# Probabilities stationary and V moving in the PV product of a decode-attention kernel

## The chip, the core and the metric

The kernel runs on one core of one Trainium2 chip. The core has five engines with in-order instruction streams of their own: TensorE (PE in the profile, with its weight loads as PEld), VectorE (DVE), ScalarE (ACT), GpSimd (POOL) and SyncE (SP, which here only issues DMAs). The metric is the device time of one execution in microseconds (us); lower is better. Times of several runs of one kernel are given by their median.

## The reference

Two rounds of the same two layers, with the same weights and the same caches in both rounds, for 8 sequences of one new token each:

```python
x = x + A(layernorm(x))      # grouped-query attention over a cache, then wo
x = x + B(layernorm(x))      # silu MLP
x = x + A(layernorm(x))
x = x + B(layernorm(x))

def A(x):                    # B=8, D=512, Hq=32, Hkv=8 (REP = 4 query heads per kv head), Sk=8192, Dh=128
    q = (x @ wq) in heads
    scores = q . k_cache * Dh**-0.5
    p = softmax(scores, over Sk)
    return (p . v_cache in heads) @ wo
```

K and V hold 8 sequences x 8 kv heads x 8192 keys x 128 values each in bf16, 2 MiB per sequence and kv head in each of K and V. Both rounds read all of them.

## The kernel before

One *task* is one round (`layer` 0 or 1), one sequence b and one kv head g: 128 tasks in all. A task has four steps of 2048 keys, so there are 512 steps, counted by `c`. A step's K and V pieces are 512 KB each, and lie in slots of an on-chip store, `ARENA`, of 28 slots (`NSLOT`). A piece has 128 partitions x 2048 values: 16 chunks of 128 keys.

Of each sequence, the K pieces of the last five kv heads (20 slots, `KEEP`) stay in the store from round 0 to round 1. The order of the tasks (`make_tasks`) therefore goes per sequence: five tasks of round 0 whose K is kept, some tasks of other rounds and sequences that load everything while the kept K occupies 20 of the slots, then the five tasks of round 1 that use the kept K and load V alone. I call the steps of these last five tasks **kept steps** (40 tasks, 160 steps in all), and the others **streaming steps**.

SP issues the loads in the order of need. A load waits until the instruction that last read its slot has finished; how far SP goes at which step is set by `issue_until`.

In a streaming step the main loop (L873 to L913) emits, in this order:

- `emit_t` twice: TensorE transposes 8 chunks of K each time into one of three PSUM banks `TPp` (L474), and ScalarE (first half, L480) or VectorE (second half, L482) copies them back over the piece
- pieces of the softmax of earlier tasks: `softmax_exp` (VectorE L520, L522, then ScalarE L524 writes the probabilities `P`), `softmax_sum` (VectorE L530, GpSimd L532), `softmax_rcp` (VectorE L549)
- `emit_pv` of step c-6 (`LAG`): P times V for a task before
- at one step in four, where c leaves the remainder 1 on division by 4: `emit_norm` (VectorE L574) of the task whose last PV has just been emitted, and `emit_pt`, which transposes the next task's `P` on TensorE (L540) and copies it into `PT` on VectorE (L544)
- `emit_s`: the scores of step c (L500). Four matmuls with the query stationary, 32 columns each, and 512 keys moving, in four column tiles of TensorE (`tile_position=(0, t * QR)`)
- `softmax_max` after the last scores of a task (VectorE L511, L513, GpSimd L515)

In a kept step there are no transposes, and the scores are emitted ahead of the PV. After the last round-0 task of each sequence a *chain* of small steps (wo, layer norm, MLP, next queries) is threaded through the following steps.

The operations of each engine run in the order in which they are emitted. `op` gives an instruction the waits for what it reads and writes, by name (`reads`, `writes`); on VectorE also those on VectorE's own earlier results.

The PV product before: the V chunk (128 keys x 128 values) is the stationary operand, and the moving operand is the chunk's probabilities of four heads, each repeated 8 times (32 columns). A step has 16 weight loads and 16 matmuls; all 64 of a task add into one small area of the PSUM bank `OTp`, which then holds the output of four heads, values on partitions. `emit_norm` is one VectorE multiplication by 1 / sum. What ends the step before the first PV of the next task is therefore one small VectorE operation.

Of the kernel before, what the change touches and what calls it, by code (L numbers as in the profile page):

```python
# [7 lines left out]
DH = 128  # L8
# [5 lines left out]
GRP = 8  # L14
HALVES = 2
SPT = 4
# [15 lines left out]
INT32 = mybir.dt.int32  # L32
ACT = mybir.ActivationFunctionType
ALU = mybir.AluOpType
AX = mybir.AxisListType
# [202 lines left out]
def _build(ctx, nc, A_x, A_k_cache, A_v_cache, A_wq, A_wo, B_w1, B_w2, out):  # L238
    B, _sq, D = A_x.shape
# [14 lines left out]
    tasks = make_tasks(B, HKV, (len(order) - KEEP) // NGRAN)  # L254
# [5 lines left out]
    pe = nc.tensor  # L260
    dve = nc.vector
# [41 lines left out]
    assert KB == D  # L303
    P = sb([128, KB], BF16, "P")
    Xr = P
    PT = sb([128, CPB, NT, NGRAN * REP], BF16, "PT")
    small = sb([128, 4 * REP + 23 * NST + 5 * B + 2 * KT + FT], FP32, "small")
    taken = [0]

    def few(n):  # L310
        o = taken[0]
        taken[0] += n
        assert taken[0] <= small.shape[-1]
        return small[:, o:o + n]

    hm, hneg, hsc, nbr = [few(REP) for _ in range(4)]
    mxr, mxa, ssm, ssa, rcp = [[few(REP) for _ in range(NST)] for _ in range(5)]
    mxp, nb, rs = [[few(1) for _ in range(NST)] for _ in range(3)]
    vr, yr, tr, s1, s1a = [few(B) for _ in range(5)]
    last_use = [max(d.free for d in loads if d.slot <= s < d.slot + d.n) for s in range(NSLOT)]  # L320
    spare = last_use.index(min(last_use))

    def apart(space, shapes):
        o, got = 0, []
        for shape, dt in shapes:
            n = math.prod(shape) * (2 if dt == FP32 else 1)
            v = space[:, o:o + n]
            o += n
            v = v.bitcast(FP32) if dt == FP32 else v
            got.append(v.rearrange("p (k b) -> p k b", b=shape[1]) if len(shape) == 2 else v)  # L330
        assert o <= space.shape[-1]
        return got
# [1 line left out]
    one = (few(KT).unsqueeze(2), few(KT).unsqueeze(2), tiny[:, 0:KT].unsqueeze(2), "1")  # L334
    eh, hsT = few(FT), tiny[:, KT:KT + FT]
    rows8 = ((KT, B), FP32), ((KT, B), FP32), ((KT, B), BF16)
    opens = tuple(apart(PT[:, :, :, :].rearrange("p c t q -> p (c t q)"), rows8)) + (None,)
    *ends, ones, ehN, thN, hsN, XF, XO = apart(
        ARENA[:, spare * SLOT:(spare + 1) * SLOT],
        rows8 + (((128,), BF16), ((FT * B,), FP32), ((FT * B,), FP32), ((FT * B,), BF16), ((KT * B,), BF16), ((KT * B,), BF16)))  # L340
# [3 lines left out]
    OTp = ps_bank("OTp")  # L344
    UP = ps_bank("UP")
    TPp = [ps_bank("TPp", BF16) for _ in range(NTP)]
# [62 lines left out]
    with nc.Block() as block:  # L409

        @block.sync
        def _(sync_eng):
# [9 lines left out]
                reads=["ident"], writes=["ident"],  # L422
            )
            for n in range(NQB):
# [4 lines left out]
                    hm[:, :], ident[:, :].rearrange("p (t r k) -> p r t k", t=NT, k=NGRAN)[:, 0:REP], AX.XY, ALU.add),  # L429
                reads=["ident"], writes=["hm"],  # L430
            )
            op(dve, lambda: dve.tensor_scalar(hneg[:, :], hm[:, :], -1.0, MASKED, op0=ALU.add, op1=ALU.mult),
               reads=["hm"], writes=["hneg"])
            op(dve, lambda: dve.tensor_scalar(hsc[:, :], hm[:, :], -SM_SCALE, None, op0=ALU.mult),
# [100 lines left out]
            def emit_pt(ti):  # L535
                tb = evacs[0] % NTP
                evacs[0] += 1
                tpv = TPp[tb][:, 0:KB].rearrange("p (c q) -> p c q", q=128)
                steps = [
                    lambda c=c: pe.transpose(tpv[:, c, :], P[:, c * 128:(c + 1) * 128], ident[:, :])  # L540
                    for c in range(CPB)
                ]
                mm_group(steps, reads=["P", "ident"], writes=[f"TP{tb}"])
                op(dve, lambda: dve.tensor_copy(  # L544
                    PT[:, :, :, :], tpv.rearrange("p c (t q) -> p c t q", q=QR)[:, :, :, 0:NGRAN * REP]), reads=[f"TP{tb}"], writes=["PT"])

            def softmax_rcp(ti):
                st = ti % NST
# [2 lines left out]
            def emit_pv(c):  # L551
                ti = c // SPT
                _l, b, g, k = where(c)
                slot = v_slot[(b, g, k)]
                otp = OTp[:, 0:REP * PVN].rearrange("p (r n) -> p r n", n=PVN)
                steps = []
                for n in range(HALVES * GRP):
                    cc = k * HALVES * GRP + n
                    steps.append(
                        lambda n=n, cc=cc: pe.matmul(  # L560
                            otp, chunk(slot, n), PT[:, cc % CPB, (cc // CPB) % NT, cc // (CPB * NT)::NGRAN].unsqueeze(2).to_broadcast([128, REP, PVN]),
                            start=(cc == 0), stop=(cc == NCH - 1),
                        )
                    )
                mm_group(steps, reads=[r_half(slot, 0), r_half(slot, 1), "PT"], writes=["OT"])

            def emit_norm(ti):
                layer, b, g = tasks[ti]
                st = ti % NST
                if layer == 0:  # L570
                    dst, rd = at1[b % 3][:, g * REP:(g + 1) * REP], f"at1_{b % 3}"
                else:
                    dst, rd = QA[:, b, g * REP:(g + 1) * REP], f"QA{b}"
                op(dve, lambda: dve.tensor_tensor(dst, OTp[:, 0:REP * PVN:PVN], rcp[st][:, :], ALU.mult),  # L574
                   reads=["OT", f"rcp{st}"], writes=[rd])

            def ln_stages(xv, rx, n, bufs):
                xcv, sqv, xnv, tag = bufs
# [235 lines left out]
            def add_rest(b):  # L814
                while heads[b]:
                    add_heads(b)
# [35 lines left out]
            last0 = {b: max(task_at[(0, b, g)] for g in range(HKV)) for b in range(B)}  # L852
            first1 = {b: min(task_at[(1, b, g)] for g in range(HKV)) * SPT for b in range(B)}
            ntask = len(tasks)
            first = min(g for g, _k in kept)

            def step(kind):
                if chain and chain[0][0] == kind:
                    chain.pop(0)[1]()
                    return True  # L860
                return False

            def soft(c, f):
                if 0 <= c < NC and c % SPT == 0:
                    f(c // SPT)
# [7 lines left out]
            for c in range(NC + LAG):  # L873
                if c < NC:
                    layer, b, g, k = where(c)
                if c and c % SPT == 0 and c < NC:
                    assert layer == 0 or not chain or chain_b[0] != b
                    emit_q(c // SPT)
                ready = c < NC and (c < SPT or layer == 1 and (g, k) in kept)
                if ready:  # L880
                    scores(c)
                else:
                    emit_t(c, 0)
                    emit_t(c, 1)
                soft(c - SPT, softmax_exp)
                soft(c - SPT - 1, softmax_sum)
                soft(c - SPT - 2, softmax_rcp)
                step(MID)
                if 0 <= c - LAG:
                    emit_pv(c - LAG)  # L890
                    if (c - LAG) % SPT == SPT - 1:
                        emit_norm((c - LAG) // SPT)
                issue_until(2 * c)
                soft(c - SPT - 1, emit_pt)
                if turn[0] == B and not chain and heads[B]:
                    add_heads(B)
# [5 lines left out]
                if c >= LAG and (c - LAG) % SPT == SPT - 1:  # L902
                    tj = (c - LAG) // SPT
                    layer, b, g = tasks[tj]
                    if layer == 0:
                        heads[b].append(g)
                    elif b == B - 1:
                        heads[B].append(g)
                    if layer == 0 and tj == last0[b]:
                        assert not chain and turn[0] == b  # L910
                        chain.extend([(TILE, lambda b=b: add_rest(b))] + chain_of(b))
                        chain_b[0] = b
                        turn[0] = b + 1  # L913
            assert not queue and not chain

            rest = closing(B)
# [37 lines left out]
```

## Time and profile before

| what | value |
|---|---|
| runs | 1150.9, 1144.49, 1144.27 us; median 1144.49 us |
| the profiled execution | 1147.56 us; its span 1145.8 us |
| granted TensorE clock, mean | 0.929 |
| DMA traffic | 459.43 MB, mean 401 GB/s |
| PV matmuls L560 | 8192, 291.9 us busy |
| PV weight loads L560 | 8192, 250.6 us busy |
| score matmuls L500 | 2048, 220.7 us busy |
| K transposes L474 | 5632, 393.8 us busy |
| normalization L574 | 128, 20.1 us busy |

The span is the time from the first to the last instruction of the profiled execution. In a line of the timeline the first number is the start (us from the span's start), the second the duration in us; then engine, line, operation, what it writes and reads with shapes, the number of merged instructions, and in brackets the idle time of the engine before it with what ended it. In a line of a group, "busy" is total time and the number after it the mean duration in ns of one instruction.

### The profile page before, as it was taken

The numbers are of one execution on the slowest core, as the hardware profiler recorded it, in microseconds if no ns is written. First come the engines' busy times: TensorE is split into PE (matmuls) and PEld (weight loads), VectorE is DVE, ScalarE is ACT, GpSimd is POOL, SyncE is SP. The second block draws the span as 40 slices with busy tenths as digits, with TensorE's granted clock in tenths as the row PEclk, the third lists the DMA queues.
The fourth block names the chain that finished last, engine by engine and source line by source line (L and its number), as shares of the span: only waits on it lengthen the run. The fifth ranks groups of instructions, "written<-read, shape, count | busy, mean of one in ns | idle before, by whom it ended". The sixth has DMA issues, their size and how long they took to land.

```text
span 1145.8 us, 42536 instructions
## 1 busy us (share of the span) xinstructions
PE 926.5 (81%) x18616; PEld 697.2 (61%) x18616; DVE 536.3 (47%) x1702; ACT 471.5 (41%) x747; POOL 117.6 (10%) x300
## 2 busy tenths in 40 slices
PE   2868888888888887888788888888878888888886
PEld 2656665666566665766466655666566655666565
DVE  1334553445534553446434553446444553456433
ACT  1344441454335542554235542554245432554332
POOL 0000111001100011001100111001100011011110
PEclk9889997899879998999889997999889998999877
DMA  9999999999999999999999999999999999999994
GB/s 371 394 395 415 395 404 416 418 412 390 414 418 415 392 405 417 418 409 395 409 419 414 369 379 418 419 410 393 415 418 415 394 407 418 417 404 396 413 418 200
DMA packets 100334, 459.43 MB, mean 401 GB/s; under 512 B 10541, under 2 KB 16437, under 8 KB 73781
## 3 DMA queue, kind: packets, MB, share of 16 engines
q1 hardware_dynamic: 100132, 456.70, 99.2%
q8 instruction: 147, 2.41, 0.9%
q14 instruction: 39, 0.31, 0.1%
q10 hardware_dynamic: 16, 0.01, 0.0%
HBM read 456.66 MB, written 0.01 MB: 399 GB/s over the span
## 4 chain that ended last, share of the span: by engine, by line
DMA 66%; PE 21%; DVE 6%; SPq 3%; issue 2%; ACT 0%; POOL 0%; POOLq 0%; ACTq 0%; DVEq 0%
DMA arena<-in_A_v_cache_dram 53%; DMA arena<-in_A_k_cache_dram 11%; PE TPp L474 10%; DVE arena L482 5%; PE OTp L560 4%; PE SCp L500 4%; SPq L378 3%; DMA wo<-in_A_wo_dram 3%; PE MISC L678 2%; PE TPp L540 0%; DVE small L549 0%; DVE small L530 0%; PE MISC L650 0%; SPq L84 0%; DVE small L520 0%
## 5 line engine op out<-in xcount | busy, mean ns | idle before, releaser
L480 ACT COPY arena<-TPp 128x1024 bf16<-128x1024 bf16 x352 | 356.2, 1012 | 448.4 <-PE TPp L474 446.0
L474 PE MATMUL TPp<-ident,arena 128*128 128x128 bf16 x5632 | 393.8, 226 | 35.4 <-DMA arena<-in_A_k_cache_dram 21.3
L482 DVE COPY arena<-TPp 128x1024 bf16<-128x1024 bf16 x352 | 243.2, 691 | 361.9 <-PE TPp L474 359.0
L474 PEld LDWEIGHTS TPp<-ident,arena 128*128 128x128 bf16 x5632 | 331.9, 101 | 131.9 <-DMA arena<-in_A_k_cache_dram 67.2
L560 PE MATMUL OTp<-PT,arena 128*128 128x32 bf16 x8192 | 291.9, 179 | 75.5 <-DMA arena<-in_A_v_cache_dram 72.2
L560 PEld LDWEIGHTS OTp<-PT,arena 128*128 128x128 bf16 x8192 | 250.6, 97 | 158.5 <-DMA arena<-in_A_v_cache_dram 129.7
L500 PE MATMUL SCp<-arena,QB 128*32 128x512 bf16 x2048 | 220.7, 421 | 76.7 <-DVE arena L482 24.9
L524 ACT ACTIVATE P<-SCp,small 128x512 bf16<-128x512 f32 x128 | 87.9, 687 | 197.9 <-DVE small L522 137.3
L511 DVE TENSOR_REDUCE small<-SCp 128x1 f32<-128x512 f32 x128 | 88.4, 691 | 109.6 <-PE SCp L500 108.5
L500 PEld LDWEIGHTS SCp<-arena,QB 128*32 128x32 bf16 x2048 | 60.9, 96 | 116.8 <-ACT arena L480 64.6
L515 POOL PARTITION_ALL_REDUCE small<-small x128 | 47.5, 371 | 594.8 <-DVE small L513 594.8
L532 POOL PARTITION_ALL_REDUCE small<-small x128 | 55.3, 432 | 347.4 <-DVE at L574 147.4
L540 PE MATMUL TPp<-ident,P 128*128 128x128 bf16 x512 | 53.3, 231 | 9.7 <-ACT P L524 9.2
L530 DVE TENSOR_SCALAR small<-small 128x4 f32<-128x4 f32 x128 | 28.5, 223 | 37.0 <-ACT P L524 37.0
L544 DVE COPY PT<-TPp 128x256 bf16<-128x256 bf16 x128 | 36.5, 285 | 10.0 <-PE TPp L540 7.9
L540 PEld LDWEIGHTS TPp<-ident,P 128*128 128x128 bf16 x512 | 31.8, 101 | 12.1 <-ACT P L524 11.9
L513 DVE TENSOR_SCALAR small<-small 128x4 f32<-128x4 f32 x128 | 29.3, 229 | 4.5
L520 DVE TENSOR_TENSOR small<-small 128x4 f32<-128x4 f32 x128 | 19.8, 155 | 20.4 <-POOL small L515 20.4
L678 PE MATMUL MISC<-wo,at 128*32 128x128 bf16 x1024 | 26.4, 233 | 3.6 <-DMA wo<-in_A_wo_dram 3.6
L691 DVE STREAM_TRANSPOSE UP<-MISC 128x128 f32<-128x128 f32 (+2 forms) x40 | 22.1, 552 | 14.8 <-PE MISC L678 14.8
L524 ACT ACTIVATION_READ_ACCUMULATOR P<-SCp,small 128x1 f32 x128 | 24.7, 193 | 0.0
L522 DVE TENSOR_REDUCE small<-small 128x1 f32<-128x4 f32 x128 | 20.1, 157 | 4.4
(67 smaller groups left out, 223.1 us busy)
## 6 DMA issues: line engine op xcount, KB each, us to landing
arena<-in_A_v_cache_dram SPq DMA_DIRECT2D x133, 1024.0 KB, 14.4
arena<-in_A_v_cache_dram SPq DMA_DIRECT2D x230, 512.0 KB, 6.5
arena<-in_A_k_cache_dram SPq DMA_DIRECT2D x214, 512.0 KB, 7.3
arena<-in_A_k_cache_dram SPq DMA_DIRECT2D x69, 1024.0 KB, 20.6
wq<-in_A_wq_dram SPq DMA_DIRECT2D x1, 4096.0 KB, 16.5
wo<-in_A_wo_dram SPq DMA_DIRECT2D x1, 4096.0 KB, 29.8
w<-in_B_w_dram SPq DMA_DIRECT2D x2, 1792.0 KB, 24.5
P<-in_A_x_dram ACTq DMA_DIRECT2D x1, 8.0 KB
```

Of the source, the lines that this page charges most:

```text
L474: lambda c=c: pe.transpose(tpv[:, c, :], chunk(slot, h * GRP + c), ident[:, :])
L480: op(act, lambda: act.copy(dst, TPp[tb][:, :]), reads=[f"TP{tb}"], writes=[r_half(slot, h)])
L482: op(dve, lambda: dve.tensor_copy(dst, TPp[tb][:, :]), reads=[f"TP{tb}"], writes=[r_half(slot, h)])
L500: lambda t=t: pe.matmul(SCp[bank][t * QR:(t + 1) * QR, :], QB[qn][:, NGRAN - 1 - k:NGRAN - 1 - k + QR], keys[:, t * KB:(t + 1) * KB], star ...
L511: op(dve, lambda: dve.tensor_reduce(mxp[st][:, :], SCp[bank][:, :], AX.X, ALU.max), reads=[f"SC{bank}"], writes=[f"mxp{st}"])
L515: op(pool, lambda: pool.partition_all_reduce(mxa[st][:, :], mxr[st][:, :], 128, bass.bass_isa.ReduceOp.max), reads=[f"mxr{st}"], writes=[f ...
L524: op(act, lambda: act.activation(P[:, :], SCp[bank][:, :], ACT.Exp, bias=nb[st][:, 0:1], scale=SM_SCALE, accum_out=rs[st][:, :]), reads=[f ...
L532: op(pool, lambda: pool.partition_all_reduce(ssa[st][:, :], ssm[st][:, :], 128, bass.bass_isa.ReduceOp.add), reads=[f"ssm{st}"], writes=[f ...
L540: lambda c=c: pe.transpose(tpv[:, c, :], P[:, c * 128:(c + 1) * 128], ident[:, :])
L544: op(dve, lambda: dve.tensor_copy(PT[:, :, :, :], tpv.rearrange("p c (t q) -> p c t q", q=QR)[:, :, :, 0:NGRAN * REP]), reads=[f"TP{tb}"], ...
L560: lambda n=n, cc=cc: pe.matmul(otp, chunk(slot, n), PT[:, cc % CPB, (cc // CPB) % NT, cc // (CPB * NT)::NGRAN].unsqueeze(2).to_broadcast([ ...
L678: lambda t=t, col=col, w=w, start=start, stop=stop: pe.matmul(MISC[t * QR:(t + 1) * QR, 0:math.prod(w.shape[1:])], spread(col), w, start=s ...
```

## The change

The probabilities become the stationary operand and V the moving one, in four column tiles, as the scores are done. V lies in a slot as four blocks of four chunks each. For each block t one matmul loads 16 columns of `PT` (four chunks x four heads) as weights and moves the block's 512 columns (four chunks x 128 values). Its output has 16 rows and 512 columns at partitions 32t to 32t+15, of which only the four diagonal blocks (chunk equal to chunk) are wanted. A task accumulates its four steps there. Then, for each task of the new form:

- `emit_fold`: four VectorE operations, each on 128 partitions x 128 fp32 values of `OTp`, times a mask column of `hm`, the last three adding into the sum. `fold` is an fp32 view of `P`'s space.
- in `emit_norm`: one fp32 matmul with `fold` stationary (128 x 128) and `pick` moving (128 x 4), which sums the rows of each head into a `TPp` bank; then the VectorE multiplication as before, reading that bank.

The fold is emitted right after `emit_pt` at the step of the task's last PV. The matmul and the multiplication are emitted one step later, ahead of the first PV of the next task; what follows from a finished task (`finished`) moves to that later step too. Nine tasks (`short`: the last round-0 task of each sequence and the last task of all) keep the old form, with its old place. `PT` is laid out with the block index ahead of the chunk index. At the start, `pick` is computed and `OTp` is set to zero.

```diff
-    PT = sb([128, CPB, NT, NGRAN * REP], BF16, "PT")
+    fold = P[:, 0:2 * DH].bitcast(FP32)
+    PT = sb([128, NT, CPB, NGRAN * REP], BF16, "PT")
...
             def emit_pv(c):
...
-                for n in range(HALVES * GRP):
+                if ti not in short:
+                    steps = [
+                        lambda t=t: pe.matmul(
+                            OTp[t * QR:t * QR + NGRAN * REP, :], PT[:, t, :, :].rearrange("p c q -> p (c q)")[:, k::NGRAN],
+                            ARENA[:, slot * SLOT + t * KB:slot * SLOT + (t + 1) * KB],
+                            start=(k == 0), stop=(k == NGRAN - 1), tile_position=(0, t * QR),
+                        )
+                        for t in range(NT)
+                    ]
+                for n in range(HALVES * GRP if ti in short else 0):
...
+            def emit_fold(ti):
+                if ti in short:
+                    return
+                for j in range(CPB):
+                    part, m = OTp[:, j * DH:(j + 1) * DH], hm[:, j:j + 1]
+                    if j == 0:
+                        op(dve, lambda: dve.tensor_scalar(fold, part, m, None, op0=ALU.mult),
+                           reads=["OT", "hm"], writes=["P"])
+                    else:
+                        op(dve, lambda: dve.scalar_tensor_tensor(fold, part, m, fold, op0=ALU.mult, op1=ALU.add),
+                           reads=["OT", "hm", "P"], writes=["P"])
+
             def emit_norm(ti):
                 layer, b, g = tasks[ti]
+                o, ro = OTp[:, 0:REP * PVN:PVN], "OT"
+                if ti not in short:
+                    tb = evacs[0] % NTP
+                    evacs[0] += 1
+                    o, ro = TPp[tb][:, 0:2 * REP].bitcast(FP32), f"TP{tb}"
+                    op(pe, lambda: pe.matmul(o, fold, pick[:, :], start=True, stop=True), reads=["P", "pick"], writes=[ro])
...
-                op(dve, lambda: dve.tensor_tensor(dst, OTp[:, 0:REP * PVN:PVN], rcp[st][:, :], ALU.mult),
-                   reads=["OT", f"rcp{st}"], writes=[rd])
+                op(dve, lambda: dve.tensor_tensor(dst, o, rcp[st][:, :], ALU.mult),
+                   reads=[ro, f"rcp{st}"], writes=[rd])
...
+            short = set(last0.values()) | {ntask - 1}
...
                 step(MID)
+                done, j = divmod(c - LAG + 1, SPT)
+                folded = done - 1 if j == 1 and done > 0 and done - 1 not in short else None
+                summed_up = done - 1 if j == 0 and done > 0 else None
+                if folded is not None:
+                    emit_norm(folded)
                 if 0 <= c - LAG:
                     emit_pv(c - LAG)
-                    if (c - LAG) % SPT == SPT - 1:
-                        emit_norm((c - LAG) // SPT)
+                    if summed_up in short:
+                        emit_norm(summed_up)
                 issue_until(2 * c)
                 soft(c - SPT - 1, emit_pt)
+                if summed_up is not None:
+                    emit_fold(summed_up)
```

More of the change, by code (lines that the diff above doesn't have):

```diff
@@ L305, in _build @@
     Xr = P
-    PT = sb([128, CPB, NT, NGRAN * REP], BF16, "PT")
-    small = sb([128, 4 * REP + 23 * NST + 5 * B + 2 * KT + FT], FP32, "small")
+    fold = P[:, 0:2 * DH].bitcast(FP32)
+    PT = sb([128, NT, CPB, NGRAN * REP], BF16, "PT")
+    small = sb([128, 5 * REP + 23 * NST + 5 * B + 2 * KT + FT], FP32, "small")
     taken = [0]
@@ L318, in _build @@
     mxp, nb, rs = [[few(1) for _ in range(NST)] for _ in range(3)]
+    pick = few(REP)
     vr, yr, tr, s1, s1a = [few(B) for _ in range(5)]
@@ L336, in _build @@
     rows8 = ((KT, B), FP32), ((KT, B), FP32), ((KT, B), BF16)
-    opens = tuple(apart(PT[:, :, :, :].rearrange("p c t q -> p (c t q)"), rows8)) + (None,)
+    opens = tuple(apart(PT[:, :, :, :].rearrange("p t c q -> p (t c q)"), rows8)) + (None,)
     *ends, ones, ehN, thN, hsN, XF, XO = apart(
@@ L431, in _ @@
             )
+            op(
+                dve,
+                lambda: dve.tensor_reduce(
+                    pick[:, :], ident[:, :].rearrange("p (t r k) -> p k t r", t=NT, k=NGRAN)[:, :, :, 0:REP], AX.XY, ALU.add),
+                reads=["ident"], writes=["pick"],
+            )
+            op(dve, lambda: dve.memset(OTp[:, :], 0.0), writes=["OT"])
             op(dve, lambda: dve.tensor_scalar(hneg[:, :], hm[:, :], -1.0, MASKED, op0=ALU.add, op1=ALU.mult),
@@ L544, in emit_pt @@
                 op(dve, lambda: dve.tensor_copy(
-                    PT[:, :, :, :], tpv.rearrange("p c (t q) -> p c t q", q=QR)[:, :, :, 0:NGRAN * REP]), reads=[f"TP{tb}"], writes=["PT"])
+                    PT[:, :, :, :].rearrange("p t c q -> p c t q"), tpv.rearrange("p c (t q) -> p c t q", q=QR)[:, :, :, 0:NGRAN * REP]), reads=[f"TP{tb}"], writes=["PT"])
             def softmax_rcp(ti):
@@ L556, in emit_pv @@
                 steps = []
-                for n in range(HALVES * GRP):
+                if ti not in short:
[4 more added lines that the diff above has]
+                            start=(k == 0), stop=(k == NGRAN - 1), tile_position=(0, t * QR),
+                        )
+                        for t in range(NT)
+                    ]
+                for n in range(HALVES * GRP if ti in short else 0):
                     cc = k * HALVES * GRP + n
@@ L560, in emit_pv @@
                         lambda n=n, cc=cc: pe.matmul(
-                            otp, chunk(slot, n), PT[:, cc % CPB, (cc // CPB) % NT, cc // (CPB * NT)::NGRAN].unsqueeze(2).to_broadcast([128, REP, PVN]),
+                            otp, chunk(slot, n), PT[:, (cc // CPB) % NT, cc % CPB, cc // (CPB * NT)::NGRAN].unsqueeze(2).to_broadcast([128, REP, PVN]),
                             start=(cc == 0), stop=(cc == NCH - 1),
@@ L861, in step, with finished @@
                 return False
+            def finished(tj):
+                layer, b, g = tasks[tj]
+                if layer == 0:
+                    heads[b].append(g)
+                elif b == B - 1:
+                    heads[B].append(g)
+                if layer == 0 and tj == last0[b]:
+                    assert not chain and turn[0] == b
+                    chain.extend([(TILE, lambda b=b: add_rest(b))] + chain_of(b))
+                    chain_b[0] = b
+                    turn[0] = b + 1
             def soft(c, f):
@@ L901, in _ @@
                 soft(c - SPT + 1, softmax_max)
[L902 to L913, printed above, removed]
+                if folded is not None:
+                    finished(folded)
+                if summed_up in short:
+                    finished(summed_up)
             assert not queue and not chain
```

## The prediction, made before the changed kernel was run

> **What bounds the kernel now.** I read the page first, then a table of busy time by stretches of 20 us, the timeline of both kinds of step, the waits, and single groups.
>
> ```profile
> PE 926.5 (81%) x18616; PEld 697.2 (61%) x18616; DVE 536.3 (47%) x1702; ACT 471.5 (41%) x747; POOL 117.6 (10%) x300
> ...
> DMA  9999999999999999999999999999999999999994
> ...
> q1 hardware_dynamic: 100132, 456.70, 99.2%
> q8 instruction: 147, 2.41, 0.9%
> ```
>
> The 16 DMA engines are full from start to nearly the end. TensorE's 81% looks far from a bound. The stretches (start:end, length, busy us of PE, PEld, DVE, ACT, POOL; clock, DMA share, GB/s) show that no stage leaves the DMA idle:
>
> ```profile
> 180.00:200.00 20.00, 16.74 (x320) 9.87 (x320) 7.50 (x32) 3.46 (x12) 3.20 (x8) 0.76 1.02 421
> 220.00:240.00 20.00, 16.98 (x364) 14.02 (x360) 9.39 (x25) 10.92 (x16) 1.60 (x4) 1.00 1.01 417
> 280.00:300.00 20.00, 17.68 (x360) 12.56 (x349) 12.79 (x43) 9.46 (x13) 2.40 (x6) 1.00 1.02 402
> ```
>
> The first is of kept steps, the other two of streaming steps. In these the share is 1.01 or 1.02 while the rate is 402 to 421 GB/s: the difference is that of the packets (kept steps load 8 KB, many streaming ones 4 KB at a time), not of idle engines. A faster TensorE alone can win little. How much slower it may become is read from the waits:
>
> ```profile
> PE OTp L560 <- DMA arena<-in_A_v_cache_dram: 72.2, 185, 3.1
> ```
>
> In the timeline, the starts of the score groups (L500) between 170 and 1129 us are 2.275 us apart in 182 of 303 streaming steps: TensorE's own pace. The other steps exceed that by 55.6 us together; 8 x 1.07 of it is the first step after each kept stretch (3.35 us). Some 47 us, about 6 for each sequence, are what TensorE can lose before DMA waits for it.
>
> Which dependence gives the 2.275 us:
>
> ```profile
> 608.30 1.07 PE L474 MATMUL TPp<-ident,arena 128*128 128x128 bf16 x16
> 609.21 0.56 PE L560 MATMUL OTp<-PT,arena 128*128 128x32 bf16 x16
> 609.41 0.69 DVE L482 COPY arena<-TPp 128x1024 bf16<-128x1024 bf16 x1 [1.19 <-PE TPp L474]
> 610.24 0.40 PE L500 MATMUL SCp<-arena,QB 128*32 128x512 bf16 x4
> ```
>
> Transposes, VectorE's copy, scores, transposes again. PV ends at 609.77, under the copy that the scores wait for (610.10). A shorter PV buys nothing here. A task of kept steps is a longer loop:
>
> ```profile
> 573.81 0.40 PE L540 MATMUL TPp<-ident,P 128*128 128x128 bf16 x4
> 574.25 0.29 DVE L544 COPY PT<-TPp 128x256 bf16<-128x256 bf16 x1 [0.17 <-PE TPp L540]
> 574.93 0.57 PE L560 MATMUL OTp<-PT,arena 128*128 128x32 bf16 x16 [0.39 <-DMA arena<-in_A_v_cache_dram]
> 575.42 0.40 PE L500 MATMUL SCp<-arena,QB 128*32 128x512 bf16 x4
> 575.88 0.69 DVE L511 TENSOR_REDUCE small<-SCp 128x1 f32<-128x512 f32 x1 [1.12 <-PE SCp L500]
> 577.77 0.69 ACT L524 ACTIVATE P<-SCp,small 128x512 bf16<-128x512 f32 x1 [3.92 <-DVE small L522]
> 578.65 0.38 PE L540 MATMUL TPp<-ident,P 128*128 128x128 bf16 x4
> ```
>
> P is transposed, PT copied, the task's first PV runs, then the last scores of a later task, whose max, exp and P follow 2.8 us later (575.82 to 578.65). One round lasts 4.74, 4.84, 5.30 and 5.00 us in four tasks: 4.97.
>
> **What the change does, part by part.**
>
> *PV itself.* 119 tasks x 4 steps lose 16 pairs of load and matmul (0.57 us) and get four in column tiles, like L500's group (0.40 us). The 0.17 us lies under the copy in streaming steps and under the softmax in kept ones: nothing on the path.
>
> *Instructions.* TensorE's 37,232 become about 26,000 (-16,384, +1,152 kept, +3,808, +238): 30% of the instruction fetch, which takes 0.9% of the DMA engines (10.3 us). That is 3.1 us, if DMA stays the bound.
>
> *Fold.* No row shows it. Nearest is L787, the same operation on 128x112 fp32 from PSUM: 275 ns. The 16 further elements add 17 ns (from there to L511's 691 ns at 512). A mask column as operand costs another 59 ns (L530 with one 223, L434 without 164). So 0.35 us each, 1.40 for four, with 0.03 of hand-over at each (L622 starts 1138.97, lasts 0.17, L623 starts 1139.17): 1.52 us. Without the operand's price: 1.29.
>
> *Sum by TensorE.* No fp32 matmul is in the trace. Bounds: four bf16 pairs 128x8 (L600) 0.28 us from first load to last end; 16 such pairs (L664) 0.60. I take 0.45, in the middle. It waits for the fold, and all of TensorE queues behind it: the first PV of the next task (so the release of V's slot, which SP waits for at its next load), then the scores.
>
> The Trainium skill, "FP8 and Floating Point Precision", section "TensorE Precision Notes", says that true fp32 takes four passes through the array. Estimated from it, four loads of 0.10 us and the 0.17 of a small matmul make 0.57 us, and 5 us more in the total; no run here shows it yet.
>
> *Kept steps.* Nothing else can run between: the scores that the next softmax needs come behind the sum in TensorE's order. The new loop: P's transposes to the end of PT's copy 0.73, fold 1.52, VectorE to TensorE 0.14 (610.10 to 610.24), sum 0.45, PV and scores behind it 0.68 (L678's 16 matmuls with 512 columns take 1.23 us, so groups follow each other by 0.28, and the last lasts 0.40), softmax 2.8. Total 6.32 instead of 4.97: +1.35 us, times 40 tasks 54 us. Bounds: 5.92 with 1.29 and 0.28; 7.1 with the clock low, as many of these steps have it now (L540 then takes 0.61, scores 0.62, and groups follow each other more slowly). So +0.95 to +2.1: 38 to 84 us. A gain is excluded: operations are only added to the loop.
>
> *Streaming steps.* At the boundary PT's copy ended at 608.22, so the fold would end at 609.77, and the copy of K's second half would start 0.36 later than 609.41. TensorE: 609.77 + 0.14 + 0.45 + 0.28 = 610.64, when the scores may start, instead of 610.24. So +0.40; bounds +0.13 (fold 1.29, sum 0.28) and +0.67 (sum 0.60, PV not overlapped, 0.40). After the first kept stretch 66 streaming tasks of the new form remain: 26 us (9 to 44).
>
> *At nothing:* the memset, `pick` (two VectorE operations under the first loads), PT's layout (same 285 ns copy of the same size), the later `finished` (its wo work slips one step; the nine old-form tasks start the chains unchanged), one more user of the three TPp banks (each is free a step later).
>
> Sum for the profiled execution: 1147.6 + 54 + 26 - 47 = 1181. The instruction saving is no gain where DMA no longer bounds. The median of the runs is 3.1 below the profiled execution: 1177.
>
> **The rivals.**
>
> *DMA stays the bound (not slower).* With the low ends the kernel adds 38 + 9 = 47 us, which the slack just holds. Then only the last kept stretch is not made up for: 5 x 0.95 us less 2.5 us of waiting for V in it (1072 to 1102 us) is +2, with -3.1 for instructions: 1147.6 - 1 = 1146.5, median 1143.5. It decides at a sum of 47 us, at about 0.95 us per kept task with 0.13 per streaming one. For it: full queues in kept stretches. Against: the fold and the sum must then both come out at their low ends.
>
> *The clock stays low in kept steps.* There it is 0.76 now, and TensorE would wait more. High ends: 84 + 44 - 40 = +88, 1233. Half of that way is as likely: 1205.
>
> *Column tiles don't run side by side.* Then a PV group lasts four times 0.21 us or more, and TensorE falls behind by about 0.3 us in every step: over 1250. L500's four matmuls last 421 ns each and 0.40 together, which speaks against it.
>
> *TensorE's saved switches matter.* Before PV in kept steps TensorE's loads stand idle 0.23 to 0.44 us ("issue").
> The Trainium skill, "TensorEngine Tiling (Array Packing)", section "Key Properties", says that a change of tiling mode drains the array; by it these gaps vanish, as scores and PV now share a mode.
> But with 40 x 4 x 0.44 us gone, DMA's 99% would still hold the time: at most 3.1 us for instructions and some 4 for the moments in which fewer than 16 packets are under way (in 10 to 1130 us): 1137.
>
> **How the numbers follow.** One per cent (11.4 us) is about what a measurement of this kernel tells from no change. The forecast, 1177, with its low-clock variant: 0.71 (0.17 of it the variant). DMA stays the bound: 0.21, within one per cent. Saved switches: 0.05, of which 0.03 are given to faster, as packets might also become quicker. Not side by side: 0.03. Faster 0.03, same 0.23 (0.21 + 0.02), slower 0.74 (0.71 + 0.03). The range reaches from the rival's 1142 to 1212, short of the clock's high end.
>
> **What would show it.** Right: score starts in kept stretches about 6.3 us apart per task, TensorE before the sum waiting for VectorE at the fold's line for more than 1 us there; waits for V nearly gone; streaming steps at 2.275 throughout but for some 2.7 at the boundary; DMA share and GB/s down by 3%. Wrong: fold operations near 0.29 us, kept tasks at 5 us, DMA still at 99%, waits for V of the same size, only q8 down to about 100 packets.

## The result, and the profile after

The changed kernel takes 1182.05 us, the median of six runs (1178.60 to 1184.81), beside 1148.01 us for six of the kernel before: a ratio of 1.029, 95% interval 1.027 to 1.032. It is slower by 34 us. Its profiled execution took 1178.63 us with a span of 1176.9, against 1145.8 before: +31.1.

From the head of its page: busy time by engine, then two DMA queues, the loads of K and V (q1) and the instruction fetch (q8).

```profile
PE 907.4 (77%) x13142; PEld 569.4 (48%) x13142; DVE 684.1 (58%) x2180; ACT 471.6 (40%) x747; POOL 117.9 (10%) x300
...
q1 hardware_dynamic: 100132, 456.70, 97.9%
q8 instruction: 104, 1.70, 0.6%
```

TensorE lost 5,474 matmuls and 19 us of busy time, instruction packets fell from 147 to 104, and VectorE gained 148 us. DMA went from 99.2% of the span to 97.9% while it moved the same bytes: it now stands idle at times. The chain of waits agrees: DMA made up 66% of it before, now 22%, with 32% on TensorE and 21% on VectorE.

The new operations, as groups (count, busy time and mean ns of one, idle time before them with its cause):

```profile
L594 DVE SCALAR_TENSOR_TENSOR P<-OTp,small,P 128x128 f32<-128x128 f32 x357 | 125.1, 351 | 12.6
L604 PE MATMUL TPp<-small,P 128*128 128x4 f32 x238 | 50.8, 284 | 73.8 <-DVE P L594 73.4
```

L594 is three of the four fold operations; the first, L591, takes 342 ns. L604 is the sum. There are 119 of it, but 238 matmuls. The two waits that matter, in us, times and longest:

```profile
PE TPp L604 <- DVE P L594: 73.4, 100, 1.8
PE OTp L568 <- DMA arena<-in_A_v_cache_dram: 24.3, 84, 1.3
```

TensorE's wait for V fell from 72.2 us to 24.3, and a wait for the fold took its place. Where it is paid shows in TensorE's timeline of one kept round at full clock (start, duration, idle time before it):

```profile
186.43 0.40 PE L549 MATMUL TPp<-ident,P 128*128 128x128 bf16 x4 [0.65 <-ACT P L533]
...
188.63 0.39 PE L604 MATMUL TPp<-small,P 128*128 128x4 f32 x2 [1.47 <-DVE P L594]
188.94 0.40 PE L568 MATMUL OTp<-arena,PT 128*16 128x512 bf16 x4
189.17 0.39 PE L509 MATMUL SCp<-arena,QB 128*32 128x512 bf16 x4
...
192.34 0.61 PE L549 MATMUL TPp<-ident,P 128*128 128x128 bf16 x4 [0.91 <-ACT P L533]
```

and, with VectorE, of one at a low clock:

```profile
587.62 0.61 PE L549 MATMUL TPp<-ident,P 128*128 128x128 bf16 x4 [0.65 <-ACT P L533]
...
588.48 0.34 DVE L591 TENSOR_SCALAR P<-OTp,small 128x128 f32<-128x128 f32 x1
588.85 1.12 DVE L594 SCALAR_TENSOR_TENSOR P<-OTp,small,P 128x128 f32<-128x128 f32 x3
...
590.03 0.59 PE L604 MATMUL TPp<-small,P 128*128 128x4 f32 x2 [1.25 <-DVE P L594]
...
590.94 0.64 PE L509 MATMUL SCp<-arena,QB 128*32 128x512 bf16 x4
...
591.63 0.69 DVE L520 TENSOR_REDUCE small<-SCp 128x1 f32<-128x512 f32 x1 [0.82 <-PE SCp L509]
...
594.37 0.61 PE L549 MATMUL TPp<-ident,P 128*128 128x128 bf16 x4 [0.65 <-ACT P L533]
```

The first round takes 5.91 us, the second 6.75. The same four matmuls of L549 tell the clocks apart: 0.40 us and 0.61. In both, TensorE waits more than a microsecond for the fold, then sum, PV and the last scores (L509) run, and only then can the max (L520) start, while VectorE waits in its turn.

From the starts of the score groups, the span in parts (us):

| part | before | after | difference |
|---|---|---|---|
| up to the first scores | 34.6 | 35.5 | +0.9 |
| from there to the first kept step, tasks 0 to 13 | 139.6 | 141.2 | +1.6 |
| eight kept stretches of 5 tasks | 245.4 | 284.5 | +39.1 |
| seven streaming stretches between them | 683.5 | 671.8 | -11.7 |
| last three tasks | 42.6 | 43.9 | +1.3 |

A kept stretch is counted up to the first scores of the streaming step behind it. The kept stretches lose 39 us, and what lies between them makes up 12. Within a kept stretch of five tasks lie four whole rounds, from P's transposes to the next ones; their mean went from 5.17 us to 6.39.

After a kept stretch the DMA rate shows how the making up ends. Windows of 20 us of the changed kernel (columns as in the prediction):

```profile
180.00:200.00 20.00, 13.81 (x121) 5.19 (x119) 10.22 (x38) 2.60 (x9) 2.82 (x7) 0.59 1.02 420
240.00:260.00 20.00, 16.61 (x250) 11.02 (x250) 12.10 (x36) 10.93 (x16) 1.98 (x5) 1.00 0.94 351
```

In the kept window the DMA is still full (420 GB/s), since loads issued ahead feed it, and the clock is 0.59 (0.76 before). In the streaming window TensorE runs at its own pace and DMA falls to a share of 0.94 and 351 GB/s; the kernel before had 1.02 and 410 there. The lateness of the kept stretch comes out here as a DMA queue that has run low.

### The profile page after: what moved, and what is told of

The parts are those of the page before. It is cut to its first block, busy times and chain, and to the rows that moved or that the text cites. A ratio compares the mean times of both kernels' runs of the same rounds, so it can differ in the third digit from the quotient of the medians.

```text
span 1176.9 us, 31868 instructions
## 1 busy us (share of the span) xinstructions
PE 907.4 (77%) x13142; PEld 569.4 (48%) x13142; DVE 684.1 (58%) x2180; ACT 471.6 (40%) x747; POOL 117.9 (10%) x300
## 3 DMA queue, kind: packets, MB, share of 16 engines
q1 hardware_dynamic: 100132, 456.70, 97.9%
## 4 chain that ended last, share of the span: by engine, by line
PE 32%; DMA 22%; DVE 21%; issue 18%; SPq 3%; POOL 2%; ACT 1%; POOLq 0%; ACTq 0%; DVEq 0%
PE TPp L483 17%; DMA arena<-in_A_v_cache_dram 13%; DVE arena L491 9%; DMA arena<-in_A_k_cache_dram 7%; PE SCp L509 6%; DVE P L594 6%; PE OTp L568 4%; SPq L380 3%; DMA wo<-in_A_wo_dram 3%; PE TPp L604 2%; DVE P L591 2%; POOL small L524 1%; PE MISC L714 1%; ACT P L533 1%; DVE PT L553 1%
## 5 line engine op out<-in xcount | busy, mean ns | idle before, releaser
L491 DVE COPY arena<-TPp 128x1024 bf16<-128x1024 bf16 x352 | 242.7, 690 | 250.2 <-PE TPp L483 247.5
L509 PE MATMUL SCp<-arena,QB 128*32 128x512 bf16 x2048 | 229.3, 438 | 77.2 <-DVE small L529 31.2
L568 PE MATMUL OTp<-arena,PT 128*16 128x512 bf16 x1904 | 217.6, 447 | 24.7 <-DMA arena<-in_A_v_cache_dram 24.3
L509 PEld LDWEIGHTS SCp<-arena,QB 128*32 128x32 bf16 x2048 | 65.2, 100 | 160.7 <-ACT arena L489 85.0
L520 DVE TENSOR_REDUCE small<-SCp 128x1 f32<-128x512 f32 x128 | 88.5, 691 | 78.5 <-PE SCp L509 77.4
L594 DVE SCALAR_TENSOR_TENSOR P<-OTp,small,P 128x128 f32<-128x128 f32 x357 | 125.1, 351 | 12.6
L604 PE MATMUL TPp<-small,P 128*128 128x4 f32 x238 | 50.8, 284 | 73.8 <-DVE P L594 73.4
L568 PEld LDWEIGHTS OTp<-arena,PT 128*16 128x16 bf16 x1904 | 52.1, 99 | 89.7 <-DMA arena<-in_A_v_cache_dram 47.1
L604 PEld LDWEIGHTS TPp<-small,P 128*128 128x128 f32 x238 | 40.8, 215 | 101.3 <-DVE P L594 101.2
L549 PE MATMUL TPp<-ident,P 128*128 128x128 bf16 x512 | 55.1, 235 | 36.0 <-ACT P L533 36.0
L549 PEld LDWEIGHTS TPp<-ident,P 128*128 128x128 bf16 x512 | 31.5, 103 | 83.1 <-ACT P L533 65.4
L591 DVE TENSOR_SCALAR P<-OTp,small 128x128 f32<-128x128 f32 x119 | 40.7, 342 | 0.0
```

Source lines behind the costliest of these rows:

```text
L491: op(dve, lambda: dve.tensor_copy(dst, TPp[tb][:, :]), reads=[f"TP{tb}"], writes=[r_half(slot, h)])
L509: lambda t=t: pe.matmul(SCp[bank][t * QR:(t + 1) * QR, :], QB[qn][:, NGRAN - 1 - k:NGRAN - 1 - k + QR], keys[:, t * KB:(t + 1) * KB], star ...
L520: op(dve, lambda: dve.tensor_reduce(mxp[st][:, :], SCp[bank][:, :], AX.X, ALU.max), reads=[f"SC{bank}"], writes=[f"mxp{st}"])
L568: lambda t=t: pe.matmul(OTp[t * QR:t * QR + NGRAN * REP, :], PT[:, t, :, :].rearrange("p c q -> p (c q)")[:, k::NGRAN], ARENA[:, slot * SL ...
L591: op(dve, lambda: dve.tensor_scalar(fold, part, m, None, op0=ALU.mult), reads=["OT", "hm"], writes=["P"])
L594: op(dve, lambda: dve.scalar_tensor_tensor(fold, part, m, fold, op0=ALU.mult, op1=ALU.add), reads=["OT", "hm", "P"], writes=["P"])
```

## The experiments

Two readings were open. Either the fold and the sum in the loop of the kept steps cost the time, by their length; or the new PV form itself, or the streaming steps, do. Later a third came: that the new wait costs through TensorE's clock. All diffs are against the changed kernel, except the second, which is against the kernel before. Line numbers in profile lines are those of each kernel; where the changed kernel has the sum at L604, the others have it within some lines of that.

**1. The new PV alone.** No fold and no sum: the normalization reads undiagonalized columns of `OTp` at its old place, so the output is not the product.

```diff
             def emit_fold(ti):
-                if ti in short:
-                    return
+                return
...
-                folded = done - 1 if j == 1 and done > 0 and done - 1 not in short else None
+                folded = None
...
-                    if summed_up in short:
+                    if summed_up is not None:
                         emit_norm(summed_up)
```

> Leaves out the fold and the sum of rows: the 119 tasks are normalized straight from four columns of OTp, so their output is not attention's. Theory (the loop of the kept steps): the loop falls back to about 4.5 us, under DMA's 5.0, kept stretches to 30 or 31 us of the 35.4 of the changed kernel, and the time to that of before or 3 us below it (fewer instructions to fetch): 1143 to 1149. Rival (PV with V moving is itself dearer, by reading V as the moving operand or by slower packets beside it): the time stays above 1165.

Measured: 1137.29 us (before, on that chip, 1146.63), below the expected range; ratio 0.9915, interval 0.9886 to 0.9944. Kept rounds 5.07 us. One of its waits:

```profile
PE OTp L568 <- DMA arena<-in_A_v_cache_dram: 92.9, 193, 1.8
```

TensorE waits for V more than before (72.2 us): DMA is the bound again. So the new PV form costs nothing by itself and gains 9 us; the fold and the sum use that up and bring all of the loss.

**2. The old PV with the fold and the sum as idle work.** The kernel before, with the same fold after `emit_pt` and the same sum ahead of the next task's first PV, for the same 119 tasks. Their result is not used.

```diff
+                tf = (c - LAG) // SPT
+                if c > LAG and (c - LAG) % SPT == 0 and tf - 1 not in short:
+                    emit_sum(tf - 1)
...
+                if c > LAG and (c - LAG) % SPT == SPT - 1 and tf not in short:
+                    emit_fold(tf)
```

> The kernel before with its old PV, to which the four fold operations and the fp32 matmul are added as idle work at the places of the changed kernel, for the same 119 tasks; nothing reads their result. Theory: about as slow as the changed kernel, 1175 to 1195, with kept stretches of 35 to 37 us, somewhat longer than with the new PV as 16 pairs last longer than four. Rival (new PV is the cause): under 1155.

Measured: 1202.43 us, above the expected range; ratio 1.0483 (1.0444 to 1.0521). Kept rounds 6.56 us, kept stretches 290.4 us in all, the seven streaming stretches 688.9. Fold and sum alone reproduce the loss without any new PV. They even cost 56 us here against the 34 of the changed kernel. Most of the difference, 17 us, lies in the seven streaming stretches: behind the sum stands the old PV's group of 0.57 us, where the new one takes 0.40. For the 64 tasks whose sum falls there, 64 x 0.17 makes 11 of them, and the steps with the sum show that: they exceed 2.275 us by 21.6 us in all, against 10.4 in the changed kernel.

**3 and 4. By place.** One kernel keeps the old form for the 40 tasks whose fold falls into kept steps; the other is the complement and has the new form for these 40 alone.

```diff
-            short = set(last0.values()) | {ntask - 1}
+            beside = {t - 2 for t in range(ntask) if tasks[t][0] == 1 and tasks[t][2] >= first}
+            short = set(last0.values()) | {ntask - 1} | beside
```

and for the complement

```diff
+            short = set(last0.values()) | {ntask - 1} | (set(range(ntask)) - beside)
```

> The 40 tasks whose normalization falls into kept steps get the old form too; 79 keep the new one. Theory: kept stretches back to 30 or 31 us, streaming boundary steps still 2.34 instead of 2.275 (4 us in all, taken up by slack): 1144 to 1152. Rival (VectorE's added 166 us or the boundary as such, in any task): only a third of the loss goes, 1170 or more.

> The complement of e3: only the 40 tasks whose normalization falls into kept steps have the new form, all others the old one. Theory: nearly the whole loss comes back, 1172 to 1184, with kept stretches of 35 us. Rival (the loss needs the folds of the streaming tasks too): under 1162.

Measured: without the fold in kept steps 1147.09 us, ratio 0.9995 (0.9968 to 1.0022), kept stretches 243.7 us; with it in kept steps alone 1175.02 us, ratio 1.0241 (1.0214 to 1.0268), kept stretches 288.8. The loss belongs to the 40 tasks in kept steps. The 79 others, on their own, cost nothing that can be told from zero; on top of the 40 they may add some 6 us (1.0293 against 1.0241, with intervals that touch).

**5. The scores ahead of the sum.** In kept steps the sum and the first PV behind it, with the loads that it releases, are put behind the next scores, and the max ahead of the normalization. Nothing is left out.

```diff
                 if ready:
                     scores(c)
...
+                due = None
+                if late is not None:
+                    due, late = late, None
+                    emit_sum(due)
+                    emit_pv(c - 1 - LAG)
+                    issue_until(2 * (c - 1))
+                    issue_until(2 * (c - 1) + 1)
+                if folded is not None and ready and c >= SPT:
...
+                    late, folded = folded, None
+                    step(TURN)
+                    continue
```

> All 119 tasks in the new form, but in kept steps the fourth scores of the task are emitted ahead of the sum of rows and the first PV of the next task, and its max ahead of the normalization on VectorE, so the next softmax no longer waits for the sum. Theory: the loop is then PT copy 0.73, fold 1.5, max to the next P 2.75, together 5.0 us, a little over it at the low clock: kept stretches 30 to 32 us, time 1144 to 1158. Rival (the cost is work or the low clock, not the order): kept stretches stay at 35 us and the time above 1170.

Measured: 1147.24 us; ratio 1.0006 (0.9984 to 1.0028); kept stretches 242.4 us. A round in the timeline:

```profile
188.26 0.40 PE L549 MATMUL TPp<-ident,P 128*128 128x128 bf16 x4 [0.78 <-ACT P L533]
...
188.59 0.62 PE L509 MATMUL SCp<-arena,QB 128*32 128x512 bf16 x8
...
190.41 0.66 DVE L520 TENSOR_REDUCE small<-SCp 128x1 f32<-128x512 f32 x1
...
190.46 0.39 PE L603 MATMUL TPp<-small,P 128*128 128x4 f32 x2 [1.25 <-DVE P L594]
```

TensorE waits as long for the fold as before (1.25 us), and the four fold operations are all there. But both score groups (x8) run ahead of that wait, and the max starts as soon as the fold leaves VectorE: the round is 4.85 us at full clock. With the same work added, the loss is gone: it hung on the scores' place behind the sum.

**6. Half a fold.** Two of the four fold operations, in place, so that half of the keys are missing in the output.

```diff
-                for j in range(CPB):
+                for j in range(CPB // 2):
```

> The changed kernel with two of the four fold operations left out, so half of the keys are missing from the sum. Theory (each microsecond between P and the scores of the kept loop is paid in full until DMA bounds): 0.70 us less in each of 40 kept tasks, 28 us in all, less the few that DMA's floor near 1140 takes back: 1152 to 1160, kept stretches 31.5 to 33 us. Rival (a low clock that the waiting brings, not the length of the fold): under half of that, above 1168.

Measured: 1143.88 us; ratio 0.9974 (0.9961 to 0.9987); kept stretches 255.6 us. TensorE's timeline:

```profile
568.34 0.61 PE L549 MATMUL TPp<-ident,P 128*128 128x128 bf16 x4 [0.65 <-ACT P L533]
...
569.98 0.59 PE L604 MATMUL TPp<-small,P 128*128 128x4 f32 x2 [0.47 <-DVE P L594]
...
574.32 0.40 PE L549 MATMUL TPp<-ident,P 128*128 128x128 bf16 x4 [0.73 <-ACT P L533]
```

A round takes 5.98 us at the low clock and 5.15 at the full one: 0.77 less than the changed kernel's at the same clock, which is two fold operations with their hand-over (2 x 0.38). The kept stretches fell by 29 us, about the 28 expected. The total fell by more, below the expected 1152 to 1160: the span is 34 us shorter, and why 5 of these lie outside the kept stretches is open. Kept stretches that take 10 us more than before cost nothing in the total.

**7. The fold as a copy.** ScalarE copies `OTp`'s 512 columns as bf16 into `P` in one operation, and the sum becomes four bf16 matmuls whose moving operand picks the diagonal blocks. Once with the order of the change, once also with the order of experiment 5.

```diff
-                for j in range(CPB):
-                    part, m = OTp[:, j * DH:(j + 1) * DH], hm[:, j:j + 1]
...
+                op(act, lambda: act.copy(P[:, :], OTp[:, :]), reads=["OT"], writes=["P"])
...
-                    op(pe, lambda: pe.matmul(o, fold, pick[:, :], start=True, stop=True), reads=["P", "pick"], writes=[ro])
+                    mm_group(
+                        [lambda j=j: pe.matmul(o, P[:, j * DH:(j + 1) * DH], pick[:, j * REP:(j + 1) * REP],
+                                               start=(j == 0), stop=(j == CPB - 1)) for j in range(CPB)],
+                        reads=["P", "pick"], writes=[ro])
```

> The fold's four VectorE operations become one ScalarE copy of the 512 columns to bf16, and the fp32 sum four bf16 matmuls that pick the diagonal blocks by a mask in their moving operand; places and order are those of the changed kernel. Theory: the loop of a kept task is 0.73 + 0.6 (copy) + 0.14 + 0.3 + 0.68 + 2.8 = 5.25 us, just over DMA's 5.0; VectorE loses its 166 us: 1138 to 1150, kept stretches 30 to 32 us. Rival (any work between P and the scores starves DMA): above 1160.

> The same with the fourth scores of a kept task ahead of the sum, as in e4: neither the copy nor the sum is left in the softmax's loop, which is then about 4.5 us, under DMA's 5.0. Theory: DMA bounds throughout, kept stretches 30 us, and most of the 9 us that PV alone gained are kept: 1136 to 1143, faster than before by 0.4 to 0.9%. Rival (what e1 gained goes with any work at the boundary): 1146 as e3 and e4.

Measured: 1143.32 us, ratio 0.9958 (0.9936 to 0.9980), and 1140.75 us, ratio 0.9953 (0.9928 to 0.9977). The copy takes 0.58 us instead of 1.50, the sum about 0.26; kept stretches are 242.7 and 242.5 us. Both beat the changed kernel clearly and the kernel before by 0.4 to 0.5%, with nothing left out. The order adds nothing measurable on top: the two intervals overlap. DMA is the bound in both (99.4% and 99.5% of the span).

**8. What the new PV gains.** Experiment 1 with idle work behind each new PV group, of about 0.4 us: once as 11 pairs of a small load and a small matmul, once as one pair with a long matmul.

```diff
+                mm_group([lambda: pe.matmul(scrap, ident[:, 0:REP], ident[:, 0:REP], start=True, stop=True)] * 11,
+                         reads=["ident"], writes=[f"TP{tb}"])
```

```diff
+                mm_group([lambda: pe.matmul(scrap, ident[:, 0:REP], wq_sb[:, 0, 0:512], start=True, stop=True)],
+                         reads=["ident", "wq"], writes=[f"TP{tb}"])
```

> The kernel without fold and sum (same output as there), with 11 pairs of a 4-column load and a 4-column matmul of the identity behind each PV group of the new form, into a bank that the next transposes overwrite: TensorE's instructions are back to about 23,400 pairs of load and matmul instead of 12,904 (18,616 before). Theory A (the 9 us below the kernel before come from fewer instructions to fetch): 1146 to 1152. Theory B (they come from V's slots being free earlier, or from the time that TensorE saves behind PV): 1136 to 1142 if it is V's slots; the padding's own time is 0.3 to 0.6 us in each step, under VectorE's copy in streaming steps.

> As e6 (fold and sum left out), but the padding behind each PV group is one load and one matmul of 512 columns: about the same 0.4 us of TensorE as the 11 pairs, with 2 instructions in place of 22. If the 7 us that e6 lost against e1 are the fetching of instructions, this kernel is back at 1136 to 1140; if they are TensorE's time, it stays at 1143 to 1147.

Measured: 11 pairs 1144.74 us, ratio 0.9984 (0.9967 to 1.0001), 143 instruction packets; one pair 1141.26 us, ratio 0.9958 (0.9942 to 0.9973), 106 packets; without either 0.9915 and 102 packets. Both times lie between what was expected for the one cause and for the other. Instruction packets and TensorE time both seem to carry a part of the 9 us. The intervals of the two touch, and in both the granted clock rose as well (0.950 and 0.973, against 0.939), so the split stays open.

**9. The clock.** The changed kernel with idle work for TensorE in kept steps: three pairs with a long matmul where TensorE waits for the fold, and one behind two of the four PV groups.

```diff
                 if folded is not None:
+                    if ready and c >= SPT:
+                        emit_pad(3)
                     emit_norm(folded)
...
                     emit_pv(c - LAG)
+                    if ready and c >= SPT and k in (3, 0):
+                        emit_pad(1)
```

> The changed kernel, with idle work for TensorE in kept steps alone: three pairs of a 4-column load and a 512-column matmul ahead of the sum, where TensorE waits for the fold (1.25 us), and one such pair behind two of the task's four PV groups; their results are not used. Theory: TensorE's idling in the new wait is what lowers its granted clock in kept steps (0.59 between 180 and 200 us against 0.76 before), and that is a part of the cost: kept rounds of 6.75 us at the low clock and 5.92 at the full one, 6.39 in the mean. With the clock held at 0.9 or more, rounds come to 5.9 to 6.0; 32 rounds x 0.45 = 14 us less, kept stretches 270 us instead of 284.5, and a median of 1164 to 1172. Rival: the low clock has another cause, or what it costs lies beside the fold: the clock stays near 0.6, or rounds stay near 6.4, the median at 1180 or, with the idle work in the way, up to 1190.

Measured: 1153.45 us (1148.35 to 1159.95); ratio 1.0059 (1.0033 to 1.0085). The window, and a round on TensorE; L588 is the idle work, L610 the sum:

```profile
180.00:200.00 20.00, 12.56 (x147) 5.21 (x139) 10.92 (x40) 3.23 (x11) 2.77 (x7) 1.00 1.02 422
```

```profile
188.37 0.40 PE L549 MATMUL TPp<-ident,P 128*128 128x128 bf16 x4 [1.29 <-ACT P L533]
...
188.92 0.81 PE L588 MATMUL TPp<-wq,ident 128*4 128x512 bf16 x3
190.57 0.39 PE L610 MATMUL TPp<-small,P 128*128 128x4 f32 x2 [0.83 <-DVE P L600]
...
194.28 0.40 PE L549 MATMUL TPp<-ident,P 128*128 128x128 bf16 x4 [1.29 <-ACT P L533]
```

The clock is 1.00 where it was 0.59, nearly every kept round takes 5.92 us (mean 6.02), and kept stretches fall from 284.5 to 264.9 us. Work that nobody needs takes 27 us off the total by the ratios to the kernel before (24 off the span of the profiled executions), more than the 10 to 18 that I expected. I had counted the four whole rounds of a stretch alone, which gave 12 us (32 x 0.37); the rest of the stretches gave another 8. Some 5 us of the span are gained outside them, 3 of these before the first kept step, where the two kernels are the same; that part I can't explain. Of the changed kernel's 39 us in kept stretches about half goes when the clock is held up, and half stays with the longer round. That the new wait is what lowers the clock is not shown: over the eight kept stretches the mean of its records is 0.68 in the changed kernel, 0.78 before and 0.94 here, but 0.64 with half a fold, whose wait is shorter, and 0.82 in experiment 5, whose wait is as long.

How much is made up, from five traces (us, against the kernel before with 245.4 and 683.5):

| kernel | kept stretches | streaming between | span |
|---|---|---|---|
| half a fold | +10.2 | -13.8 | -3.1 |
| changed, with idle work | +19.5 | -13.3 | +6.7 |
| changed | +39.1 | -11.7 | +31.1 |
| new form in kept steps alone | +43.4 | -14.0 | +29.6 |

The stretches between make up some 12 to 14 us, about 2 for each sequence, whether 10 or 43 have been lost. What lies beyond that is nearly all of the cost. A further 12 us are made up on the way out of the kept stretches, and are already taken off in their column (see "Slack" below).

## Why the prediction was right, point by point

The forecast of 1177 was 5 us short of 1182, and its case, that fold and sum in the loop of the kept steps outrun the slack, is what the experiments show. But its sum, 54 + 26 - 47 = +33, met +31 by errors that cancel: that it came so near is luck. Each term:

- **Fold, 1.52 us.** Four operations of 342 and 351 ns, 1.50 us with hand-over. Right, and so was the operand's price in it.
- **Sum, 0.45 us.** It lasts 0.39 us at full clock and 0.59 at the low one, as two pairs of a 215 ns load and a 284 ns matmul. The estimate of 0.57 from the four passes of the Trainium skill ("FP8 and Floating Point Precision", "TensorE Precision Notes") was too high at full clock; the trace records two pairs and shows no four passes.
- **The loop, 6.32 us.** The mean of 6.39 is close, yet it is a mean of rounds from 5.92 (full clock) to 6.75 (low clock), and neither end is the one that I had built:

| part of the round | predicted | full clock | low clock |
|---|---|---|---|
| P's transposes to the start of the sum | 2.39 | 2.20 | 2.41 |
| sum to the start of PV | 0.45 | 0.31 | 0.52 |
| PV and last scores, to their end | 0.68 | 0.62 | 1.03 |
| softmax to the next transposes | 2.80 | 2.78 | 2.79 |
| round | 6.32 | 5.91 | 6.75 |

- **Kept steps, +54 us.** About right, at +51. The four whole rounds of a stretch grew by 1.22 each (5.17 to 6.39, where I had 4.97 from four rounds of one stretch), and 32 x 1.22 = 39. The fifth sum of each stretch stands between its last transposes of P and its last scores: in all eight, 14.1 us before and 26.1 after, 12 more. The +39 in the table of parts is these 51 less 12 that the way out of the stretches makes up (see "Slack").
- **The clock.** I had it as a variant with 0.17 of the chance, at 1205 to 1233. It came: the mean over the kept stretches went from 0.78 to 0.68, and what the low clock costs there is about 20 us. One reason why it did not reach those prices is that the rounds at full clock were 0.41 shorter than mine, so the mean round met 6.32 with the clock's cost in it. (Its high end takes off 40 us of slack where the sum takes off 47.)
- **Streaming steps, +26 us.** This failed, and is about 5. The boundary step in the timeline:

```profile
622.76 0.34 DVE L591 TENSOR_SCALAR P<-OTp,small 128x128 f32<-128x128 f32 x1
623.00 1.07 PE L483 MATMUL TPp<-ident,arena 128*128 128x128 bf16 x16
623.14 1.12 DVE L594 SCALAR_TENSOR_TENSOR P<-OTp,small,P 128x128 f32<-128x128 f32 x3
624.18 0.68 DVE L491 COPY arena<-TPp 128x1024 bf16<-128x1024 bf16 x1
```

The copy starts 0.11 us after the transposes end (624.07), where I had 0.40. The fold began before them and its last record ends 0.19 after them, the copy starting 0.08 earlier still, as the record of each VectorE operation begins some 0.08 us before the one ahead of it ends. One reason is in the diff: the normalization (0.16 us) no longer stands ahead of PT's copy in that step. The sum and PV then ran beside the copy, and the scores started at 625.01, 2.34 us after those before; 67 such steps x 0.07 make 5.
- **Slack, -47 us.** This is the step that failed: the kernel made up about 25. I had summed the excess over 2.275 us in all streaming steps without asking what ended each wait, and taken it all for time that DMA had set. In the seven streaming stretches the excess (without the step behind a kept stretch) was 52 us before and still 40 after, and TensorE's waits that DMA ended there only fell from 38 us to 30. Outside the kept stretches the span fell by 8 us, the boundaries' 5 included: 13. The other 12 lie in a step that I had not counted, from the last scores of a kept stretch to the first of the streaming one. In the kernel before, TensorE waits there for K and for V:

```profile
201.53 1.89 PE L474 MATMUL TPp<-ident,arena 128*128 128x128 bf16 x16 [0.79 <-DMA arena<-in_A_k_cache_dram]
...
204.01 0.61 PE L560 MATMUL OTp<-PT,arena 128*128 128x32 bf16 x16 [0.59 <-DMA arena<-in_A_v_cache_dram]
```

In the changed kernel, which arrives later, these waits are gone: the eight such steps took 42.1 us before and 30.3 after, with 13.1 us of waiting for DMA in them before and none after. So kept and streaming steps were priced 3 and 21 us too high, against 22 of relief that did not come: that is how the sum came out right.
- **PV at nothing.** Wrong, to the good: alone, the new PV gained 9 us where I had at most 3.1 for instructions, as experiment 1 shows, and how the 9 divide is open (experiment 8). In the changed kernel it is used up.
- **The saved switches.** The tile mode is now the same for PV and scores. In kept steps at full clock a PV group now starts 0.21 us after the scores ahead of it (189.17 and 189.38), where before it was 0.33 (570.64 and 570.97). The Trainium skill, "TensorEngine Tiling (Array Packing)", "Key Properties", says that a change of tiling mode drains the array. The shorter distance fits that, but PV also went from sixteen pairs to four, and no run here tells the two apart. In the changed kernel it came to nothing, as the loop waits for the fold.
- **What would show it.** TensorE's wait of over 1 us at the fold, the round near 6.3 and DMA's rate down 3% (401 to 390 GB/s) came; the waits for V fell to a third, not to nearly nothing; the boundary step was at 2.34, not 2.7.

## What to carry to other kernels

Price a new operation by what stands behind it in its engine's order: here 2 us of fold and sum for each task cost 34 us in all, and moving the next scores ahead of them in kept steps left out no work and gave it all back. The granted clock can double such a cost: look at it in the stage that has become the bound, and try idle matmuls in the wait to tell its share from that of the length. Slack is counted from the waits that the bound ends, not from the excess of the steps over the best one.

## What was not expected of the hardware

- Idle work raises the clock that TensorE is granted: 0.59 in the 20 us window of the changed kernel and 1.00 in the same window with idle matmuls (0.76 in the kernel before). The Trainium skill, "TensorE: Matmul & The Clock Gate", "Part 1: The HAM clock gate (the "warmup" mystery)", says that the throttled state is the default and that activity releases it. These two runs agree.
- The records of the granted clock hold only two values, 1.0 and 0.5, in pieces of about 3.4 us or multiples of it (20.5 us at 0.5 from 582.2 us on in the changed kernel). A figure such as 0.59 is a mean over such pieces.
- One fp32 matmul of 128x128 by 4 columns is recorded as two pairs of load and matmul, 0.39 us in all.
- Each VectorE record begins up to 0.1 us before the one ahead of it ends (624.18 and 624.26 above), so a row of short operations takes a little less time than the sum of its records.
